# Unread products in TensorE's planned gaps, single-slot weight decoding and a newly set order in a fused attention and feed-forward kernel

## The chip, the cores and the metric

The kernel runs on one core of one Trainium2 chip. The metric is the device time of one execution in microseconds (us); for the kernel before it is given as the median of three runs. The core's engines run side by side, each through its own list of instructions in order: TensorE (products), VectorE, ScalarE, GpSimd, and SyncE (SP), which issues all transfers here. They meet at semaphores.

## The reference

The input is 4 batches of 8 heads, 576 positions, 64 values per head. Three parts follow each other:

```
scores = q k^T / 8 - slope_h * |i - j|,  kept where 0 <= i - j < 128
x      = softmax(scores) v                       -> 2304 tokens x 512
h      = x w_in (512 x 1024);  e = softmax(h);  s = h * e
ln     = (s - mean(s)) / sqrt(var(s) + 1e-6) * g_ln
y      = ln w_out (1024 x 512)
h2     = y w2_in (512 x 2048);  g = h2 * sigmoid(h2)
out    = g w2_out (2048 x 512)
```

The weights arrive as 64-bit floats, 8 bytes for each value: w_in is 4.2 MB, w_out 4.2 MB, w2_in and w2_out 8.4 MB each.

## The kernel before

**Tiling.** The 2304 tokens are 18 blocks of 128. A block runs through attention in four pairs of heads: scores (`a_qk`, L615), bias and row maximum on VectorE (`a_max`, L640), exponentials on ScalarE (L645), a split of the result into a high and a low 16-bit half, a transpose, and the product with v (`a_av`, L692). `a_evac` gathers the block's 128x512 result `xm`, which is split and transposed into `xT`. `m1_in` (L734) multiplies by w_in, `layer_norm` does both normalisations, and every second block `m1_out` (L826) multiplies 256 tokens by w_out into `y16`. A pair of blocks is a chunk `c`; its last part is eight steps `j` of `m2_in` (L863), a gate (ScalarE L872, VectorE L873, ScalarE L875, VectorE L876, into a buffer `g`), and `m2_out` (L890). Every large product is made of three 16-bit products (high by high, high by low, low by high).

**Weights.** A weight is loaded in slots of 128 x 512 values, 48 in all: 8 of w_in, 8 of w_out, 16 of w2_in, 16 of w2_out. `load_weight` takes two slots at a time: two loads of 512 KB into one of `N_STAGE` = 2 stage buffers, then `decode`, three VectorE operations over 1024 elements that build 32-bit floats out of the two halves of the 64-bit ones (L414, L416, L418). The intermediate `bits` lies in PSUM, in the pool `ps_early`, two banks wide. Per slot, ScalarE (or GpSimd) squares the result and, save for w2_out, TensorE sums over partitions with a matrix of ones (L459); from the sums comes one scale for a weight. `split_weight` then makes the two 16-bit halves of each slot, by one of three ways given in the string `E_W`: V (ScalarE, VectorE L482), G (ScalarE, ScalarE, GpSimd) or H (GpSimd L487, ScalarE, GpSimd). All slots of a weight must be decoded before its scale is known. The first `m2_in` needs all of w2_in, the first `m2_out` all of w2_out.

**Transposes.** The string `ON_PE` says for each block whether the transposes of attention weights ("a"), of `xm` ("x") and of the LayerNorm result ("l") are made by TensorE (P: products with the unit matrix L520, ScalarE L522, VectorE L523) or by transfers (D: a ScalarE copy L335 or L790, a difference on VectorE L339 or GpSimd L340, transposing transfers). `ENG` says which engine takes those differences (V, G, or B for whichever ends sooner by the plan) and the normalisation ("n", V or A for VectorE L774 or ScalarE L772).

**Order.** All instructions are first recorded as `Op` objects with their dependences, a cost and a priority. `Sched.solve` then walks through a planned time: it takes the engine that can begin first and gives it the ready operation of the lowest priority number. That fixes the order on each engine and the order of buffer use; the chip then follows that order, waiting where an operand is late. The priorities come from tables: `RANK` and `PITCH` by kind and block, `WAT` by weight. The constants `N_...` say how many buffers of each kind rotate; `AHEAD` says how many steps `m2_in` is recorded ahead of `m2_out`. The planned costs are fixed numbers, with one speed for TensorE.

Of the kernel before, what the change touches and what calls it, by code (L numbers as in the profile page):

```python
# [7 lines left out]
F32 = mybir.dt.float32  # L8
# [3 lines left out]
U32 = mybir.dt.uint32  # L12
# [5 lines left out]
P = 128  # L18
# [52 lines left out]

class Sched:
    def __init__(self):
        self.ops, self.state, self.prio, self.pred = [], {}, 0.0, {}

    def at(self, kind, i, p=0):

# [100 lines left out]
    def solve(self):  # L178
# [34 lines left out]
        while n_left:  # L213
            while todo:
                o = todo.pop()
                if o.eng is None and o.turn is not None and o.fn is not None:
                    o.turn.waiting.append(o)
                    n_left -= give(o.turn)
                elif o.eng is None:
                    o.start = o.end = o.ready  # L220
                    n_left -= 1
                    settle(o)
                    if o.turn is not None:
                        turn = o.turn
                        turn.done[o.buf.place] = o.end
                        while len(turn.released) - turn.n in turn.done:
                            turn.released.append(turn.done.pop(len(turn.released) - turn.n))
                        n_left -= give(turn)
                else:
                    for alt in o.alts:  # L230
                        avail[alt[0]].append((o, alt))
            if not n_left:
                break
            best = None
            for e, lst in avail.items():
                lst[:] = [x for x in lst if not x[0].done]
                if not lst:
                    continue
                t = max(free[e], min(o.ready for o, _ in lst))
                if best is None or t < best[0]:  # L240
                    best = (t, e)
            assert best is not None, "tiles wait for each other"
            t, e = best
            o, alt = min((x for x in avail[e] if x[0].ready <= t), key=lambda x: (x[0].prio, x[0].idx))

            for other in o.alts:
                begins = max(free[other[0]], o.ready, port if other[3] else 0)
                if begins + other[1] < max(t, port if alt[3] else 0) + alt[1]:
                    alt = other
            o.eng, o.cost, o.fn, held = alt  # L250
            t = max(free[o.eng], o.ready, port if held else 0)
            o.done, o.start = True, t
            free[o.eng] = t + o.cost
            if held:
                port = t + o.cost
            if o.dma:
                dma_free = max(dma_free, t + (1100 if o.cost < 600 else 1275)) + o.dma
                o.end = dma_free
            else:
                o.end = free[o.eng]  # L260
            n_left -= 1
            settle(o)
# [33 lines left out]
def fused_kernel(ctx, tc, qk, qn, kn, vt, rel, w_in, w_out, g_ln, w2_in, w2_out, out):  # L296
# [71 lines left out]

    def over_partitions(x, n, first=False):

        pt = Buf(ps_early, [P, 1024], F32, "bits", 1) if first else Buf(ps, [P, 512], F32, "mm", 2, free=True)
        pe(220, lambda: T.matmul(pt[:, 0:n], ones.tile, x.tile, start=True, stop=True), [ones, x], [pt])
        return pt


    def norm_scale(name, parts, n=None):
# [24 lines left out]
        return big, scl  # L401


    def decode(st, slots):

        t = Buf(ps_early, [P, 2, 512], U32, "bits", 1)

        def flat(x):
            return x.rearrange("p a c -> p (a c)")

        def out():
            return W.tile.bitcast(U32)[:, slots[0]:slots[1] + 1:slots[1] - slots[0], :]
        w = [(W, sl) for sl in slots]
        v(1050, lambda: V.tensor_scalar(flat(t.tile), flat(st[:, :, :, 1]), 3, 0x3FFFFFFF, ALU.logical_shift_left,  # L414
                                        ALU.bitwise_and), [st], [t])
        v(1050, lambda: V.scalar_tensor_tensor(out=flat(t.tile), in0=flat(st[:, :, :, 1]), scalar=0xC0000000,  # L416
                                               in1=flat(t.tile), op0=ALU.bitwise_and, op1=ALU.bitwise_or), [st, t], [t])
        v(1050, lambda: V.scalar_tensor_tensor(out=out(), in0=st[:, :, :, 0], scalar=29, in1=t.tile,  # L418
                                               op0=ALU.logical_shift_right, op1=ALU.bitwise_or), [st, t], w)

    scales, sums = {}, {}

    def load_weight(name, w, slot0, n, cols, gain=None, columns=False, by_rows=False):
# [2 lines left out]
        groups = n if by_rows else nf if columns else 1  # L426
        acc = Buf(const, [P, groups], F32, "acc" + name)
        view = w.bitcast(U32).rearrange("(k p) (f e) -> p k f e", p=P, f=nf)
        for at in range(0, n, 2):
            s.prio = WEIGHT(slot0, at) - 8  # L430
            st = Buf(early, [P, 2, 512, 2], U32, "stage", N_STAGE)
            slots = []
            for z in range(2):
                f, k = divmod(at + z, n // nf)
                slots.append(slot0 + LAG + k * nf + f)
                load(512, lambda f=f, k=k, z=z, st=st: SP.dma_start(st[:, z].rearrange("p c e -> p (c e)"),
                                                                    view[:, k, f, :]), [], [(st, z)])
            s.prio = WEIGHT(slot0, at)
            decode(st, slots)

            def go(at, k, sl):
                if by_rows:
                    junk = Buf(early, [P, 512], BF16, "sq", 2)
                    act(512, lambda: A.activation(junk.tile, W[:, sl, :], AF.Square, accum_out=acc[:, at:at + 1]),
# [16 lines left out]
                if at % size == size - 1:  # L461
                    v(512, lambda: V.tensor_reduce(acc[:, at // size:at // size + 1], c.tile, AX.X,
                                                   ALU.max if columns else ALU.add), [c], [(acc, at // size)])
            for z in range(2):
                go(at + z, (at + z) % (n // nf), slots[z])
        scales[name] = norm_scale(name, acc, None if by_rows else groups)

    def split_weight(name, slot0, n, cols, per_k=None):
# [484 lines left out]
    n = 0  # L953
    for c in range(NB // 2 + 1):
# [16 lines left out]

PITCH = 3.3
RANK = {"table": -104.3, "vnorm": -66.9, "vload": 632.4, "vsplit": 82.3, "load": -243.6, "qk": -57.4,
        "max": -161.5, "exp": 217.8, "parts": -218.7, "aturn": -111.4, "av": 179.9, "evac": -188.6,
        "xturn": -57.5, "in": -119.2, "max1": 91.3, "norm": -233.0, "lparts": -421.0, "out": -334.0,
        "share": -317.7, "y": -192.5, "in2": 186.3, "gate": -449.4, "out2": 257.1, "store": -337.1}

WAT = {0: (65.8, 0.0, 85.1, 0.0), 8: (-155.1, 0.0, -336.6, 0.0), 16: (49.3, 0.0, 5.2, 0.0),
       32: (144.1, 0.0, -16.4, 0.0)}


def WEIGHT(slot0, at, split=False):
# [4 lines left out]
LAG = 2  # L992
NSLOT = 48
TB = 256
E_W = "GHGVHGVHGVVGVVHGVHVHVGGVGVGGGGGVHGVGHHVGHVGGHVVH"

ENG = {"n": "VAAAAAVVVVVAAAAAAA", "a": "GGGGGGGGVVVVVVVBVV", "x": "BGGGGVGBBBBBGGGBBB",
       "l": "VBBGGGGGBBBBBBGVVV"}

ON_PE = {"a": "DDDDPDDDDDDDDDDDDD", "x": "PDPDPPDDDDDDDDDDDD", "l": "DPDDDDDDDDDDDDDDDD"}  # L1000
N_STAGE = 2
N_VS = 2
N_VRAW = 2
N_K = 2
N_Q = 2
N_E = 2
N_A16 = 2
N_AT = 2
N_XT = 1
N_E1 = 1  # L1010
N_L16 = 1
N_LNT = 1
N_Y = 1
N_T = 6
N_G = 5
AHEAD = 1
SKEW = 0
NQ = NB
V_AT = [0, 1, 5, 9]

# [1 line left out]
_INS = ["qk", "qn", "kn", "vt", "rel", "moe_w_in", "moe_w_out", "moe_g_ln", "moe2_w_in", "moe2_w_out"]  # L1022
# [50 lines left out]
```

## Time and profile before

| quantity | value |
| --- | --- |
| median of 3 runs | 750.63 us (747.43 to 752.69) |
| profiled execution, its own time | 750.25 us |
| its span, first to last instruction | 748.5 us |
| mean granted TensorE clock | 0.962 of full |
| TensorE products: busy, share, count | 685.3 us, 92%, 5382 |
| VectorE: busy, share, count | 450.9 us, 60%, 1167 |
| ScalarE: busy, share, count | 400.5 us, 54%, 850 |
| GpSimd: busy, share, count | 111.7 us, 15%, 96 |

Busy time is the sum of an engine's instructions on the chip, not of its waiting. TensorE's products are pipelined and may overlap, so a group of several takes less time than its count times the mean of one. The granted clock is the share of full speed that the chip allows TensorE. In the rows, PE is TensorE, DVE is VectorE, ACT is ScalarE, POOL is GpSimd; `sa<-k,q` reads "writes tile sa from tiles k and q"; what stands in brackets or after `<-` with a line number is the instruction waited for. A row of the table of stretches gives, for each engine, busy us and in brackets the number of instructions that began there.

### The profile page before, as it was taken

The numbers are of one execution on the slowest core, as the hardware profiler recorded it, in microseconds if no ns is written. First come the engines' busy times: TensorE is split into PE (matmuls) and PEld (weight loads), VectorE is DVE, ScalarE is ACT, GpSimd is POOL, SyncE is SP. The second block draws the span as 40 slices with busy tenths as digits, with TensorE's granted clock in tenths as the row PEclk, the third lists the DMA queues.
The fourth block names the chain that finished last, engine by engine and source line by source line (L and its number), as shares of the span: only waits on it lengthen the run. The fifth ranks groups of instructions, "written<-read, shape, count | busy, mean of one in ns | idle before, by whom it ended". The sixth has DMA issues, their size and how long they took to land.

```text
span 748.5 us, 13814 instructions
## 1 busy us (share of the span) xinstructions
PE 685.3 (92%) x5382; PEld 458.8 (61%) x5382; DVE 450.9 (60%) x1167; ACT 400.5 (54%) x850; POOL 111.7 (15%) x96
## 2 busy tenths in 40 slices
PE   2475777989999999999999999999999999999998
PEld 1233344776766558765666677757667767857853
DVE  3899899989868884887716655641552362222220
ACT  5597758998598864666714464431432352232231
POOL 2075321443276110100000100000100000000000
PEclk9996757899999999999999999999999999999999
DMA  9899996477864652847612235121210300200000
GB/s 244 281 301 235 221 258 207 140 156 173 167 122 107 146 125 51 151 105 152 154 29 43 62 81 85 29 57 23 42 36 15 57 29 4 54 29 1 2 28 29
DMA packets 139809, 79.22 MB, mean 106 GB/s; under 512 B 121696, under 2 KB 122336, under 8 KB 139744
## 3 DMA queue, kind: packets, MB, share of 16 engines
q1 hardware_dynamic: 139744, 78.34, 44.6%
q8 instruction: 42, 0.69, 0.4%
q14 instruction: 23, 0.19, 0.1%
HBM read 44.24 MB, written 4.72 MB: 65 GB/s over the span
## 4 chain that ended last, share of the span: by engine, by line
PE 80%; DVE 8%; DMA 5%; ACT 3%; issue 2%; POOL 1%; SPq 0%; DVEq 0%; ACTq 0%
PE mm L890 25%; PE mm L863 23%; PE mm L826 13%; PE mm L734 11%; PE sa L615 4%; PE sa L692 3%; DVE bits L416 1%; DVE W L418 1%; DVE e L640 1%; DMA stage<-in_moe_w_out_dram 1%; DVE bits L414 1%; DMA stage<-in_moe_w_in_dram 1%; DMA k<-in_kn_dram 1%; DMA lnT<-ln 1%; DMA aT<-a 1%
## 5 line engine op out<-in xcount | busy, mean ns | idle before, releaser
L863 PE MATMUL mm<-y,W 128*128 128x256 f16 x1728 | 210.4, 273 | 1.8 <-DVE t L873 1.8
L890 PE MATMUL mm<-W,g 128*128 128x512 f16 x864 | 207.5, 379 | 0.0
L863 PEld LDWEIGHTS <-W 128*128 128x128 f16 x1728 | 165.9, 98 | 39.3 <-issue 2.6
L890 PEld LDWEIGHTS <-g 128*128 128x128 f16 x864 | 82.5, 98 | 74.9 <-issue 0.2
L826 PE MATMUL mm<-lnT,W 128*128 128x256 f16 x864 | 110.0, 277 | 2.3 <-DVE aT L523 1.5
L734 PE MATMUL mm<-W,xT 128*128 128x512 f16 x432 | 103.2, 391 | 2.4 <-DVE W L482 0.9
L826 PEld LDWEIGHTS <-W 128*128 128x128 f16 x864 | 84.5, 99 | 22.8 <-DVE aT L523 1.8
L645 ACT ACTIVATE e<-e,mx 128x256 f32<-128x256 f32 (+1 forms) x144 | 70.1, 488 | 43.1 <-DVE mx L640 38.4
L876 DVE SCALAR_TENSOR_TENSOR g<-t,g 128x512 f16<-128x512 f32 x72 | 50.9, 708 | 59.9 <-ACT g L875 59.7
L875 ACT ACTIVATE g<-t 128x512 f16<-128x512 f32 x72 | 45.1, 627 | 75.8 <-PE mm L890 63.5
L872 ACT ACTIVATE t<-mm,cs 128x512 f32<-128x512 f32 x72 | 48.7, 679 | 60.1 <-PE mm L863 59.9
L873 DVE SCALAR_TENSOR_TENSOR t<-t,mm 128x512 f32<-128x512 f32 x72 | 48.9, 683 | 51.3 <-ACT t L872 50.9
L615 PE MATMUL sa<-k,q 64*128 64x128 f32 x544 | 58.4, 335 | 20.9 <-DVE mx L640 14.9
L734 PEld LDWEIGHTS <-xT 128*128 128x128 f16 x432 | 42.4, 100 | 52.8 <-issue 8.8
L615 PEld LDWEIGHTS sa<-k,q 64*128 64x128 f32 x544 | 42.7, 214 | 46.6 <-DVE mx L640 25.9
L640 DVE CUSTOM_DVE_ANT_0 e<-sa,table 128x256 f32<-128x256 f32 (+1 forms) x144 | 55.1, 401 | 26.5 <-PE sa L692 13.8
L692 PEld LDWEIGHTS <-aT 128*128 128x128 f16 x816 | 33.8, 102 | 20.7 <-DMA aT<-a 9.4
L692 PE MATMUL sa<-vs,aT 128*128 128x64 f16 x816 | 37.9, 200 | 8.5 <-DMA aT<-a 4.8
L335 ACT ACTIVATE a<-e 128x512 f16<-128x512 f32 (+1 forms) x68 | 40.3, 597 | 8.7 <-DMA aT<-a 7.8
L834 DVE SCALAR_TENSOR_TENSOR y<-mm,cs,y 128x512 f16<-128x512 f32 x18 | 13.5, 750 | 49.2 <-ACT y L831 49.2
L340 POOL TENSOR_TENSOR a<-e,a 128x512 f16<-128x512 f32 (+1 forms) x28 | 31.1, 1114 | 75.3 <-ACT a L335 74.7
L340 POOL TENSOR_TENSOR W<-W 128x512 f16<-128x512 f32 x31 | 37.7, 1230 | 25.8 <-ACT W L335 25.8
(133 smaller groups left out, 685.5 us busy)
## 6 DMA issues: line engine op xcount, KB each, us to landing
stage<-in_moe_w_in_dram SPq DMA_DIRECT2D x24, 512.0 KB, 6.0
stage<-in_moe_w_out_dram SPq DMA_DIRECT2D x24, 512.0 KB, 4.9
vraw<-in_vt_dram SPq DMA_DIRECT2D x34, 256.0 KB, 4.0
k<-in_kn_dram SPq DMA_DIRECT2D x18, 256.0 KB, 2.9
q<-in_qn_dram SPq DMA_DIRECT2D x18, 256.0 KB, 3.4
out_dram<-t SPq DMA_DIRECT2D x18, 256.0 KB, 2.0
aT<-a SPq DMA_TRANSPOSE x68, 3.5
lnT<-ln SPq DMA_TRANSPOSE x34, 3.2
```

The source lines that it names most:

```text
L340: "G": ("G", cg(n), lambda: G.tensor_tensor(dst(), a(), b(), op), True)}
L615: T.matmul(SA[:, j, sl * P:(sl + 1) * P], q[rows, p, :], k[rows, p, :], start=True, stop=sl not in blank)
L640: v(n + 20, lambda j=j: V.tensor_tensor_reduce(e[:, j, lo:lo + n], SA[:, j, lo:lo + n], table[:, 2 * p + j, o:o + n], -0.125, 3.0e38, ALU. ...
L645: act(n, lambda j=j: A.activation(e[:, j, lo:lo + n], e[:, j, lo:lo + n], AF.Exp, bias=mx[:, j:j + 1], scale=-1.0, accum_out=rs[:, 2 * p + ...
L692: T.matmul(heads()[:, h // 4, h % 4, :], t[:, (2 * ha + j) * nh + c, :], vb[sl][:, h, hv, :], start=(n == 0), stop=(n == 3 * nh - 1))
L734: T.matmul(pt[:, half * 512:(half + 1) * 512], x[:, hx, k, :], W16(2 * k + half, hw), start=(k == 0 and hx + hw == 0), stop=(k == KD - 1 a ...
L826: T.matmul(pt[:, ct % 2], W16(8 + k, hw)[:, ct * P:(ct + 1) * P], l[:, hx * KF1 + k, :], start=(k == 0 and hw + hx == 0), stop=(k == KF1 - ...
L863: T.matmul(pt[:, mm], W16(16 + 4 * k + m // 4, hw)[:, (m % 4) * P:(m % 4 + 1) * P], y[:, hx, k, :], start=(k == 0 and hw + hx == 0), stop= ...
L872: act(512, lambda: A.activation(t.tile, flat(pt.tile), AF.Tanh, scale=cs[:, 0:1]), [pt, (cs, 0)], [t], extra=1)
L873: v(512, lambda: V.scalar_tensor_tensor(out=t.tile, in0=t.tile, scalar=1.0, in1=flat(pt.tile), op0=ALU.add, op1=ALU.mult), [t, pt], [t])
L876: v(512, lambda: V.scalar_tensor_tensor(out=flat(g[:, 1]), in0=t.tile, scalar=2.0 ** -16, in1=flat(g[:, 0]), op0=ALU.mult, op1=ALU.subtrac ...
L890: T.matmul(pt.tile, g[:, hg, mm, b * P:(b + 1) * P], W16(32 + m, hw), start=(m == 0 and hg + hw == 0), stop=(m == KF2 - 1 and hg == 1))
```

## The change

`solve` gets a filler. Where TensorE's next planned operation begins more than 360 ns after the last one ends, it puts products of 160 ns planned time into the gap, each a matrix of ones by 384 columns of the bias table, into a bank `idle` that is never read; only between 14 and 135 us of planned time. Weights are decoded slot by slot: one load, three VectorE operations over 512 elements, `bits` one bank wide; the bank given up is `idle`. `N_STAGE` becomes 3 buffers of half the size. The tables of priorities, the engine strings and the numbers of buffers are set anew.

```diff
 class Sched:
-        self.ops, self.state, self.prio, self.pred = [], {}, 0.0, {}
+        self.ops, self.state, self.prio, self.pred, self.filler = [], {}, 0.0, {}, None
...
             t = max(free[o.eng], o.ready, port if held else 0)
+            if o.eng == "PE" and self.filler:
+                fn, buf, (begin, end, gap) = self.filler
+                x = max(free["PE"], begin)
+                while x + gap < min(t, end):
+                    f = Op((("PE", 160, fn, False),), 0, len(self.ops))
+                    f.eng, f.cost, f.fn = "PE", 160, fn
+                    f.start, f.end = x, x + 160
+                    order.append(f)
+                    x += 160
...
-        pt = Buf(ps_early, [P, 1024], F32, "bits", 1) if first else Buf(ps, [P, 512], F32, "mm", 2, free=True)
+        pt = Buf(ps_early, [P, 512], F32, "bits", 1) if first else Buf(ps, [P, 512], F32, "mm", 2, free=True)
...
+    idle = Buf(ps_early, [P, 512], F32, "idle", 1)
+    s.filler = (lambda: T.matmul(idle[:, :3 * P], ones.tile, table[:, 0, :], start=True, stop=True), idle, FILL)
...
-    def decode(st, slots):
-        t = Buf(ps_early, [P, 2, 512], U32, "bits", 1)
...
-        v(1050, lambda: V.tensor_scalar(flat(t.tile), flat(st[:, :, :, 1]), 3, 0x3FFFFFFF, ALU.logical_shift_left,
-                                        ALU.bitwise_and), [st], [t])
...
+    def decode(st, sl):
+        t = Buf(ps_early, [P, 512], U32, "bits", 1)
+        v(512, lambda: V.tensor_scalar(t.tile, st[:, :, 1], 3, 0x3FFFFFFF, ALU.logical_shift_left,
+                                       ALU.bitwise_and), [st], [t])
+        v(512, lambda: V.scalar_tensor_tensor(out=t.tile, in0=st[:, :, 1], scalar=0xC0000000, in1=t.tile,
+                                              op0=ALU.bitwise_and, op1=ALU.bitwise_or), [st, t], [t])
+        v(512, lambda: V.scalar_tensor_tensor(out=W[:, sl, :].bitcast(U32), in0=st[:, :, 0], scalar=29, in1=t.tile,
+                                              op0=ALU.logical_shift_right, op1=ALU.bitwise_or), [st, t], [(W, sl)])
...
-        for at in range(0, n, 2):
-            st = Buf(early, [P, 2, 512, 2], U32, "stage", N_STAGE)
+        for at in range(n):
+                st = Buf(early, [P, 512, 2], U32, "stage", N_STAGE)
+                load(512, lambda: SP.dma_start(st.tile.rearrange("p c e -> p (c e)"), view[:, k, f, :]), [], [st])
+                decode(st, sl)
...
-PITCH = 3.3
-RANK = {"table": -104.3, "vnorm": -66.9, "vload": 632.4, "vsplit": 82.3, "load": -243.6, "qk": -57.4,
-        "max": -161.5, "exp": 217.8, "parts": -218.7, "aturn": -111.4, "av": 179.9, "evac": -188.6,
-        "xturn": -57.5, "in": -119.2, "max1": 91.3, "norm": -233.0, "lparts": -421.0, "out": -334.0,
-        "share": -317.7, "y": -192.5, "in2": 186.3, "gate": -449.4, "out2": 257.1, "store": -337.1}
-WAT = {0: (65.8, 0.0, 85.1, 0.0), 8: (-155.1, 0.0, -336.6, 0.0), 16: (49.3, 0.0, 5.2, 0.0),
-       32: (144.1, 0.0, -16.4, 0.0)}
+PITCH = 4.97
+RANK = {"table": -102.1, "vnorm": 36.7, "vload": 424.7, "vsplit": -53.8, "load": -121.4, "qk": -82.0,
+        "max": -49.1, "exp": 275.4, "parts": -273.2, "aturn": -68.2, "av": 137.6, "evac": -309.3,
+        "xturn": -302.2, "in": -252.9, "max1": 65.4, "norm": -154.9, "lparts": -445.6, "out": -180.2,
+        "share": -370.7, "y": -115.0, "in2": 44.4, "gate": -242.7, "out2": 166.7, "store": -203.8}
+WAT = {0: (70.8, 0.0, 124.5, 0.0), 8: (-123.5, 0.0, -241.4, 0.0), 16: (28.8, 0.0, 102.9, 0.0),
+       32: (126.1, 0.0, -0.7, 0.0)}
...
-E_W = "GHGVHGVHGVVGVVHGVHVHVGGVGVGGGGGVHGVGHHVGHVGGHVVH"
-ENG = {"n": "VAAAAAVVVVVAAAAAAA", "a": "GGGGGGGGVVVVVVVBVV", "x": "BGGGGVGBBBBBGGGBBB",
-       "l": "VBBGGGGGBBBBBBGVVV"}
-ON_PE = {"a": "DDDDPDDDDDDDDDDDDD", "x": "PDPDPPDDDDDDDDDDDD", "l": "DPDDDDDDDDDDDDDDDD"}
-N_STAGE = 2
+E_W = "HGHHHGGGVGGVHGVVVVHGHHGGVGGGGGVGVVGGGVHHVVHHGVHH"
+ENG = {"n": "VVVAAAAAAVVAVVVVVA", "a": "GGGGGGGGGGBBGGBBGB", "x": "VGGGGGGVBVBVBBGGVV",
+       "l": "GBBBBBBBGGGGGGBBVV"}
+ON_PE = {"a": "DDDDDDDDDDDDDDDDDD", "x": "PDPPDDDDDDDDDDDDDD", "l": "DPDPPDDDDDDDDDDDDD"}
+N_STAGE = 3
...
-N_Q = 2      -N_E = 2      -N_A16 = 2   -N_AT = 2    -N_XT = 1
+N_Q = 1      +N_E = 3      +N_A16 = 1   +N_AT = 3    +N_XT = 3
-N_Y = 1      -N_T = 6      -N_G = 5     -AHEAD = 1
+N_Y = 2      +N_T = 7      +N_G = 3     +AHEAD = 2
...
+FILL = (14000, 135000, 360)
```

## Rows read from the trace of the kernel before

**Rows 1.** the page's 40 slices of 18.7 us: busy tenths, and the granted clock
```profile
PE   2475777989999999999999999999999999999998
...
DVE  3899899989868884887716655641552362222220
...
PEclk9996757899999999999999999999999999999999
```

**Rows 2.** the table of stretches: the first row names the columns
```profile
core 0: us, PE busy (x) PEld busy (x) DVE busy (x) ACT busy (x) POOL busy (x), PEclk, DMA share, GB/s
0.00:30.00 30.00, 9.57 (x46) 5.62 (x47) 15.87 (x44) 17.17 (x53) 5.32 (x16) 1.00 0.89 258
30.00:130.00 100.00, 67.43 (x479) 37.60 (x477) 94.27 (x225) 74.14 (x170) 37.63 (x31) 0.76 0.94 250
130.00:205.00 75.00, 69.68 (x639) 53.13 (x640) 67.43 (x160) 61.63 (x140) 29.19 (x24) 0.96 0.70 159
205.00:500.00 295.00, 293.94 (x2505) 194.97 (x2503) 192.67 (x563) 172.61 (x378) 37.48 (x25) 1.00 0.46 95
```

**Rows 3.** TensorE's order of time: start, us taken, line, tiles, count
```profile
22.59 1.23 PE L615 MATMUL sa<-k,q 64*128 64x128 f32 x8
...
130.46 13.28 PE L826 MATMUL mm<-lnT,W 128*128 128x256 f16 x96 [1.49 <-DVE aT L523]
...
187.26 0.72 PE L615 MATMUL sa<-k,q 64*128 64x128 f32 x8 [0.18 <-DVE mx L640]
```

**Rows 4.** waits of VectorE, first 30 us: total us, times, longest
```profile
DVE bits L414 <- DMA stage<-in_moe_w_in_dram: 3.4, 3, 2.7
DVE e L640 <- PE sa L615: 3.0, 2, 2.0
```

**Rows 5.** waits of VectorE, 30 to 130 us
```profile
DVE e L640 <- PE sa L692: 3.4, 2, 2.5
DVE e L640 <- PE sa L621: 0.8, 1, 0.8
DVE bits L414 <- DMA stage<-in_moe_w_out_dram: 0.6, 1, 0.6
```

**Rows 6.** the chain that ended last, in order of time: start, us, what
```profile
624.87 6.55 PE mm L826 x60
```

**Rows 7.** the table of stretches again, another cut
```profile
14.00:135.00 121.00, 79.15 (x534) 44.92 (x535) 112.42 (x279) 88.13 (x207) 44.04 (x38) 0.78 0.91 244
```

**Rows 8.** VectorE's order of time, around 61 us and 70 us
```profile
61.05 1.22 DVE L414 TENSOR_SCALAR bits<-stage 128x1024 uint32<-128x1024 uint32 x1
62.30 1.23 DVE L416 SCALAR_TENSOR_TENSOR bits<-stage,bits 128x1024 uint32<-128x1024 uint32 x1
63.44 0.68 DVE L462 TENSOR_REDUCE accwout<-mm 128x1 f32<-128x512 f32 x1
64.04 0.69 DVE L705 TENSOR_TENSOR xm<-sa,rinv 128x512 f32<-128x512 f32 x1
...
69.59 0.75 DVE L482 SCALAR_TENSOR_TENSOR W<-W,gs 128x512 f16<-128x512 f32 x1
70.26 1.22 DVE L416 SCALAR_TENSOR_TENSOR bits<-stage,bits 128x1024 uint32<-128x1024 uint32 x1
```

**Rows 9.** groups by line and shape: total us, mean ns, idle before
```profile
L339 DVE TENSOR_TENSOR ln<-e,ln 128x1024 f16<-128x1024 f32 x11 | 13.5, 1223 | 25.7 <-ACT ln L790 25.7
...
L482 DVE SCALAR_TENSOR_TENSOR W<-W,sw2in 128x512 f16<-128x512 f32 x6 | 5.2, 861 | 0.0
...
L774 DVE TENSOR_SCALAR e<-e,lnst 128x1024 f32<-128x1024 f32 x6 | 4.9, 811 | 0.1
...
L487 POOL TENSOR_SCALAR W<-W,swin 128x512 f32<-128x512 f32 x3 | 4.6, 1564 | 0.9 <-DVE swin L400 0.9
...
L523 DVE TENSOR_TENSOR aT<-mm,aT 128x512 f16<-128x512 f32 x4 | 2.7, 683 | 0.2 <-ACT aT L522 0.2
...
L482 DVE SCALAR_TENSOR_TENSOR W<-W,swin 128x512 f16<-128x512 f32 x2 | 2.4, 1192 | 0.0
```

More of the change, by code (lines that the diff above doesn't have):

```diff
@@ L401, in norm_scale @@
         return big, scl
-    def decode(st, slots):
-        t = Buf(ps_early, [P, 2, 512], U32, "bits", 1)
[L408 to L413, printed above, removed]
-        v(1050, lambda: V.tensor_scalar(flat(t.tile), flat(st[:, :, :, 1]), 3, 0x3FFFFFFF, ALU.logical_shift_left,
-                                        ALU.bitwise_and), [st], [t])
[L416 to L419, printed above, removed]
+    def decode(st, sl):
[6 more added lines that the diff above has]
+                                              op0=ALU.logical_shift_right, op1=ALU.bitwise_or), [st, t], [(W, sl)])
     scales, sums = {}, {}
@@ L428, in load_weight, with go @@
         view = w.bitcast(U32).rearrange("(k p) (f e) -> p k f e", p=P, f=nf)
-        for at in range(0, n, 2):
-            s.prio = WEIGHT(slot0, at) - 8
-            st = Buf(early, [P, 2, 512, 2], U32, "stage", N_STAGE)
[L432 to L441, printed above, removed]
+        for at in range(n):
+            f, k = divmod(at, n // nf)
+            def go(k=k, f=f, at=at, sl=slot0 + LAG + k * nf + f):
+                s.prio = WEIGHT(slot0, at) - 8
+                st = Buf(early, [P, 512, 2], U32, "stage", N_STAGE)
+                load(512, lambda: SP.dma_start(st.tile.rearrange("p c e -> p (c e)"), view[:, k, f, :]), [], [st])
+                s.prio = WEIGHT(slot0, at)
+                decode(st, sl)
                 if by_rows:
@@ L463, in go @@
                                                    ALU.max if columns else ALU.add), [c], [(acc, at // size)])
-            for z in range(2):
-                go(at + z, (at + z) % (n // nf), slots[z])
+            go()
         scales[name] = norm_scale(name, acc, None if by_rows else groups)
@@ L1004 @@
 N_K = 2
[L1005 to L1009, printed above, removed]
+N_Q = 1
+N_E = 3
+N_A16 = 1
+N_AT = 3
+N_XT = 3
 N_E1 = 1
@@ L1012 @@
 N_LNT = 1
[L1013 to L1016, printed above, removed]
+N_Y = 2
+N_T = 7
+N_G = 3
+AHEAD = 2
 SKEW = 0
```

## The prediction

> **What bounds the kernel now.** I read the page's forty slices first. TensorE is short of work until about slice 9 and full from there to the end; VectorE is the reverse [rows 1]. The table of stretches puts numbers on it [rows 2]: TensorE is busy 9.57 us of the first 30, 67.43 of the next 100, 69.68 of the 75 after that, and then 293.94 of 295. VectorE is busy 94.27 us of the 100 from 30 to 130. So there are two regimes. From about 130 us on, TensorE sets the time, and its work there is fixed by the sizes. Before that, VectorE sets it: it decodes weights and serves attention, and TensorE takes what it is handed. The end moves only if more TensorE work is behind us when the second regime starts, or if it starts earlier.
>
> The same table shows the clock. [...]
>
> The profiled execution took 750.25 us, of which the span is 748.5; the median of the runs is 750.63, so the sum holds for the median within 0.4 us. One per cent, about what a measurement can tell from no change, is 7.5 us.
>
> **The parts, one by one.**
>
> Clock. [...] In the first 30 us that is 3.0 us (scores) [rows 4]; from 30 to 130 us it is 3.4 + 0.8 = 4.2 us [rows 5]. At full clock a score group loses 0.51 of 1.23 us, two fifths, but a saved moment also lets later work through earlier. I take 1 of the 3.0 and 3 of the 4.2 (bounds: nothing, and all 7.2). Where TensorE is already the bound, the clock counts in full: the first 96 products of m1_out took 13.28 us from 130.46 us on [rows 3], and 60 later ones 6.55 us, so 10.48 for 96 [rows 6]: 2.8 us, taken whole. Together -6.8.
>
> Fillers. A product of 384 columns costs, from 6.55/60 for 256 columns, 0.164 us at full clock and twice that at half. TensorE is idle 121 - 79.15 = 41.9 us between 14 and 135 us [rows 7], room for 255 of them, and for more once the products shrink. They need no operand that is late and write a bank that nobody reads. Laid into planned gaps they cost nothing as long as the true gap is as long; the cover is VectorE's being late. If it is gone, see the first rival. In the sum: 0 (bounds 0 and +11).
>
> Decoding slot by slot. Two pairs of numbers stand in VectorE's order of time [rows 8]. A decode operation over 1024 starts 1.25 us before one that depends on it (61.05 to 62.30) and 1.14 before one that does not (62.30 to 63.44); one over 512 is followed after 0.60 us (63.44 to 64.04) or 0.67 (69.59 to 70.26). Three operations over a pair take 3.42 us when other work stands between them and 3.64 when they follow each other (twice 1.25, once 1.14). Six over 512 take 3.6 (0.60 each) to 4.3 (0.67, and 0.11 more for the four that depend on the one before). The difference is 0.18 us at least and 0.65 with the ends crossed; for the 16 pairs of w_in, w_out and w2_in that is 3 to 10 us before TensorE is full. I take 5, nearer to the low end, because the order often puts other work between. [...] For the other eight pairs the price falls later, where TensorE is already nearly full, and I take none. In return the first decode needs one transfer landed, not two: VectorE waited 3.4 us for weights in the first 30 [rows 4]; I take 2 (bounds 0 and 3.4). Three stage buffers of one slot hold less ahead than two of two, but after that start VectorE waited for weights 0.6 us in 100 [rows 5], so 0. The loads were single slots before; their number on SP's queue is unchanged.
>
> Who does what. VectorE's part of the weight splits falls by two slots in w_in (1.19 us each), two in w2_in (0.86 each), one more in w2_out, late. Block 4's transposed weights leave TensorE and so four conversions of 0.68 on VectorE. Block 0's LayerNorm difference goes from VectorE (1.22) to GpSimd. Two more blocks are normalised on VectorE (0.81 each), and block 3's LayerNorm transposes come to TensorE (two conversions of 0.68) [rows 9]. Sum: -2.4 - 1.7 - 2.7 - 1.2 + 1.6 + 1.4 = -5.0 (bounds -5 and 0, should the other engines be late instead). On the transfer queue block 4 adds four transposes and block 5 one, block 3 takes one plus two away and block 4 two: nothing net. GpSimd is busy 37.63 of 100 us [rows 2], and gets one pre-scaling more in w_in (1.56) and two more differences; that chain leads to the first m1_in, which is covered while VectorE still has w_out to decode. If not, +4.
>
> Buffers and order. Deeper xT, aT, e and y, shallower q, a16 and g. The gaps of TensorE between 130 and 205 us are 75 - 69.68 = 5.3 us; I take -1 (bounds +5 and -5). Afterwards m2_in runs two steps ahead of m2_out instead of one, so each gate has a step more time, and three g buffers hold those two and the one being read; with one step ahead TensorE lost 1.06 us in 295 [rows 2]. The late regime keeps its length, with 4 transposes less in 5382 products.
>
> **Sum:** -6.8 + 0 + 5 - 2 - 5 - 1 = -9.8, 750.25 - 9.8 = 740 us.
>
> **Rivals.**
>
> First, slower: the fillers stand in front of real work. TensorE takes its queue in order, so a score product that is ready earlier than planned waits for the rest of its gap; VectorE stands behind it with its whole queue, the decode included. Price: where TensorE was full (130 to 205) VectorE idled 7.6 of 75 us, in 30 to 130 only 5.7 of 100 [rows 2]. At the former rate the 121 us of filling cost 12.2 instead of 6.9, so 5.4 more; as planned times also miss, I double it: 11 us, and without the gains 761 us. For it: nearly all gaps get filled, and the queue cannot pass over. Against: VectorE runs at its limit, so its answers come late rather than early, and score groups shrink by 0.5 us. It decides when VectorE's idle time from 30 to 130 us exceeds about 10 us. With dearer decoding (+5) it reaches 766.
>
> Second, nothing: VectorE is so full that the warm clock only lengthens TensorE's true idling, and the extra 72 decode operations eat the lighter splits. Then only the 2.8 us of the burst and 2 at the start are left, against +5 more from decoding: about 750 us, 744 to 757. For it: 94.27 us busy in 100. The case in which fillers do not hold the clock at all (the 360 ns left in each gap, products waiting besides) ends here too.
>
> Third, more: every favourable bound at once, because the new order lets finer pieces fill VectorE's idle time. That is -10.0 for the clock (7.2 + 2.8), +3 for decoding, -3.4 for the first load, -5.0 for the shift of work and -5.3 for TensorE's gaps: -20.7, so 729.6 us. For it: VectorE still idles 14.1 us in the first 30. Against: the page shows few waits that end on something the change touches, and the weights of the first two stages, which the change still decodes on VectorE, come first in any order.
>
> **Numbers.** Forecast (732 to 743) 0.43; more (below 732) 0.09; nothing (743 to 758) 0.28; slower (over 758) 0.20. The time is the forecast's, 740. The range 722 to 759 holds the forecast, the second rival and the third, with 7 us for what an order set anew may find besides; outside lie 0.02 below and most of the slower rival above, some 0.17. The forecast's own range is 732 to 743. Faster by over 1% (below 743): 0.43 + 0.09 = 0.52; within 1%: 0.28; slower: 0.20.
>
> **What would show it.** Right: clock 0.9 or more from 30 to 130 us; eight scores in about 0.75 us from 20 us on; the first 96 products of m1_out in under 11 us and starting no later than 130 us; VectorE over 93% busy before that; TensorE full afterwards. Decode operations over 512 of 0.64 to 0.75 us. Wrong: TensorE full of fillers while VectorE waits on scores (first rival); m1_out starting after 135 us at full clock (second); starting before 120 us (third); TensorE gaps after 205 us, which would mean that the shallower g or a16 binds.

## The result, and the profile after

The changed kernel takes 755.06 us (median; 752.91 to 756.11) against 750.93 for the kernel before on the same chips: a ratio of 1.0057 with an interval of 1.0044 to 1.0071, slower by 4 us and so within 1%. The forecast was 740, faster by over 1%. The stated range of 722 to 759 holds the time; the direction was wrong. The profiled execution took 753.98 us with a span of 752.2, 3.7 us more than the span before, and its granted clock is 1.000.

The page's slices after (busy tenths in 40 slices, then the granted clock) answer to [rows 1]:

```profile
PE   4998988888999999999999999999999999999997
DVE  5899999899887555545554444575447545321221
PEclk9999999999999999999999999999999999999999
```

TensorE now looks full from the second slice on, and the granted clock reads 0.9 or more in all 40 slices. (Lines of after are two higher than before's for the products: scores L617, attention weights times v L694, m1_in L736, m1_out L828. The decode is L421, L423, L425, the a16 copy on ScalarE L344, the difference on GpSimd L349.) The table of stretches, with the columns of [rows 2], shows what it is full of; the second fence is the same table for the unread products alone.

```profile
0.00:30.00 30.00, 19.21 (x120) 11.04 (x121) 18.99 (x55) 18.99 (x56) 3.66 (x14) 1.00 0.87 259
30.00:130.00 100.00, 89.63 (x698) 50.33 (x697) 93.78 (x244) 68.39 (x152) 41.36 (x34) 1.00 0.93 238
130.00:205.00 75.00, 67.54 (x623) 50.07 (x621) 70.12 (x192) 62.93 (x148) 33.91 (x28) 1.00 0.73 171
205.00:500.00 295.00, 292.95 (x2433) 199.09 (x2430) 167.21 (x490) 160.97 (x341) 59.12 (x44) 1.00 0.38 80
```

```profile
30.00:130.00 100.00, 50.26 (x271) 25.45 (x270) 1.00 0.93 238
```

From 30 to 130 us, 50.26 of TensorE's 89.63 us are unread products; the real work is the other 39.4 us (427 products), where it was 67.43 at the lower clock (479 products). VectorE is as busy as before (93.78 against 94.27). Behind 130 us TensorE idles more than before: 7.5 us against 5.3 in 75, and 2.05 against 1.06 in 295 [rows 2].

TensorE's order of time answers to [rows 3]:

```profile
22.40 0.71 PE L617 MATMUL sa<-k,q 64*128 64x128 f32 x8
...
63.44 0.72 PE L617 MATMUL sa<-k,q 64*128 64x128 f32 x8
...
128.87 10.19 PE L828 MATMUL mm<-lnT,W 128*128 128x256 f16 x90
139.07 5.34 PE L736 MATMUL mm<-W,xT 128*128 128x512 f16 x24
144.25 0.82 PE L828 MATMUL mm<-lnT,W 128*128 128x256 f16 x6
...
148.48 0.51 PE L694 MATMUL sa<-vs,aT 128*128 128x64 f16 x12 [1.88 <-DVE mx L642]
```

Eight scores take 0.71 us at 22 us already. The first m1_out begins at 128.87 instead of 130.46, and 90 of its products take 10.19 us, where 96 took 13.28; the last six come behind an m1_in. VectorE's waits, in total us, times and longest, answer to [rows 4, 5]; first those of the first 30 us, then those from 30 to 130:

```profile
DVE nrmb L403 <- PE mm L381: 1.1, 1, 1.1
DVE e L642 <- PE sa L617: 1.0, 1, 1.0
DVE bits L421 <- DMA stage<-in_moe_w_in_dram: 0.5, 1, 0.5
DVE e L642 <- PE sa L694: 0.4, 1, 0.4
```

```profile
DVE xm L707 <- PE sa L694: 2.2, 2, 1.6
...
DVE bits L421 <- DMA stage<-in_moe_w_out_dram: 0.6, 1, 0.6
...
DVE e L642 <- PE sa L617: 0.4, 1, 0.4
```

The waits before `e` that I wanted to see go mostly went: from 3.0 to 1.4 us in the first 30 and from 4.2 to 0.4 in the next 100. Others on TensorE came, 1.1 us before `nrmb` and 2.2 before `xm`; all of VectorE's waits on TensorE in these 130 us are 5.1 us, and were 7.2. The groups by line and shape answer to [rows 8, 9]:

```profile
L423 DVE SCALAR_TENSOR_TENSOR bits<-stage,bits 128x512 uint32<-128x512 uint32 x48 | 33.2, 693 | 0.5
L421 DVE TENSOR_SCALAR bits<-stage 128x512 uint32<-128x512 uint32 x48 | 33.1, 689 | 1.8 <-DMA stage<-in_moe_w_in_dram 0.8 <-DMA stage<-in_moe_w_out_dram 0.6
L425 DVE SCALAR_TENSOR_TENSOR W<-stage,bits 128x512 uint32<-128x512 uint32 x48 | 32.8, 683 | 0.7
```

Every mark that I named for "right" is there but the last, TensorE full afterwards, and the kernel is slower. To see where the time went I counted, in both traces, the real products still to come at a given moment and priced each kind at its mean spacing at full speed (256 columns 6.55/60 = 0.109 us [rows 6], 512 columns 0.216, a score 0.077, a product of attention weights and v 0.029, a transpose 0.125). What is left of the span beyond that work is loss.

| from the first m1_out to the end | before | after |
| --- | --- | --- |
| it begins at | 130.5 us | 128.9 us |
| span still to run | 618.0 | 623.3 |
| real work still to do | 597.2 | 599.7 |
| the rest: gaps, slow clock | 20.8 | 23.6 |

After starts this regime 1.6 us earlier, but with 2.5 us more work in front of it (24 more products of attention weights, 8 more scores, 8 more transposes) and 2.8 us more loss, although 2.8 of before's loss was the slow clock of the burst (the table reads 0.50 from 128 to 132 us, 0.51 from 132 to 136 and 1.00 from 136 to 140): 2.5 + 2.8 - 1.6 = 3.7, the difference of the spans. Attention also ends later: the last scores run at 569 us instead of 446, and from 300 to 600 us TensorE is busy 297.51 us against 299.70. That the late gaps come from the long attention is read from the traces, not tested.

### The profile page after: what moved, and what is told of

Same layout as the page of the kernel before. It is cut to its first block, busy times and chain, and to the rows that moved or that the text cites. A ratio compares the mean times of both kernels' runs of the same rounds, so it can differ in the third digit from the quotient of the medians.

```text
span 752.2 us, 14513 instructions
## 1 busy us (share of the span) xinstructions
PE 717.2 (95%) x5707; PEld 476.9 (63%) x5707; DVE 451.1 (60%) x1206; ACT 400.1 (53%) x855; POOL 148.3 (20%) x127
## 4 chain that ended last, share of the span: by engine, by line
PE 71%; DMA 8%; DVE 8%; ACT 7%; POOL 3%; issue 2%; SPq 0%; POOLq 0%; DVEq 0%; ACTq 0%
PE mm L892 24%; PE mm L865 21%; PE mm L828 11%; PE mm L736 9%; DMA aT<-a 5%; PE sa L617 3%; PE sa L694 2%; POOL a L349 1%; DMA lnT<-ln 1%; DVE e L642 1%; ACT a L344 1%; PE idle L387 1%; ACT W L344 1%; DVE bits L421 1%; POOL W L489 1%
## 5 line engine op out<-in xcount | busy, mean ns | idle before, releaser
L349 POOL TENSOR_TENSOR a<-e,a 128x512 f16<-128x512 f32 (+1 forms) x55 | 61.2, 1112 | 331.5 <-ACT a L344 331.2
L828 PE MATMUL mm<-lnT,W 128*128 128x256 f16 x864 | 103.3, 273 | 0.0
L736 PE MATMUL mm<-W,xT 128*128 128x512 f16 x432 | 98.0, 379 | 1.2 <-DMA xT<-x 0.7
L828 PEld LDWEIGHTS <-W 128*128 128x128 f16 x864 | 83.0, 98 | 17.7 <-issue 0.5
L736 PEld LDWEIGHTS <-xT 128*128 128x128 f16 x432 | 41.8, 98 | 50.1 <-issue 2.2
L642 DVE CUSTOM_DVE_ANT_0 e<-sa,table 128x256 f32<-128x256 f32 (+1 forms) x144 | 54.6, 402 | 20.8 <-POOL a L349 9.1
L387 PE MATMUL idle<-table,ones 128*128 128x384 bf16 x329 | 62.9, 333 | 0.0
L617 PE MATMUL sa<-k,q 64*128 64x128 f32 x544 | 51.8, 305 | 10.5 <-DVE mx L642 5.4
L344 ACT ACTIVATE a<-e 128x512 f16<-128x512 f32 (+1 forms) x72 | 43.0, 598 | 34.0 <-DMA aT<-a 33.8
L617 PEld LDWEIGHTS sa<-k,q 64*128 64x128 f32 x544 | 37.5, 190 | 31.3 <-DVE mx L642 10.9
L387 PEld LDWEIGHTS <-ones 128*128 128x128 bf16 x329 | 31.4, 99 | 27.4 <-issue 8.2
L750 DVE TENSOR_REDUCE lnst<-mm 128x1 f32<-128x1024 f32 x18 | 22.0, 1222 | 40.6 <-PE mm L736 40.5
L349 POOL TENSOR_TENSOR W<-W 128x512 f16<-128x512 f32 x34 | 41.1, 1221 | 10.3 <-ACT W L344 10.3
```

Of the source, the lines that this page charges most:

```text
L344: "A": ("A", ca(n), lambda: A.activation(dst(), src(), AF.Copy), False)}
L349: "G": ("G", cg(n), lambda: G.tensor_tensor(dst(), a(), b(), op), True)}
L387: s.filler = (lambda: T.matmul(idle[:, :3 * P], ones.tile, table[:, 0, :], start=True, stop=True), idle, FILL)
L617: T.matmul(SA[:, j, sl * P:(sl + 1) * P], q[rows, p, :], k[rows, p, :], start=True, stop=sl not in blank)
L642: v(n + 20, lambda j=j: V.tensor_tensor_reduce(e[:, j, lo:lo + n], SA[:, j, lo:lo + n], table[:, 2 * p + j, o:o + n], -0.125, 3.0e38, ALU. ...
L736: T.matmul(pt[:, half * 512:(half + 1) * 512], x[:, hx, k, :], W16(2 * k + half, hw), start=(k == 0 and hx + hw == 0), stop=(k == KD - 1 a ...
```

## The experiments

All ratios are against the kernel before; to put one in us, multiply by 751.

### The unread products alone

**e1** is the changed kernel without them; every other engine's list is the same.

```diff
-    s.filler = (lambda: T.matmul(idle[:, :3 * P], ones.tile, ...), idle, FILL)
+    s.filler = None
```

> The changed kernel with its order and its decoding, without the 329 unread products. Three theories. A, absorbed: VectorE bounds the first 130 us, so a full clock mostly lengthens TensorE's waits, and the 72 extra decode operations use up what is left; B, obstruction: the unread products hold up real ones; C, tables: the new priorities, engine strings and buffer numbers are the worse ones. A: the clock falls to about 0.76 between 30 and 130 us again, and the time rises by what the full clock is worth where TensorE is the bound, 2 to 6 us: ratio 1.009 to 1.014. B: it falls to or below that of the kernel before: ratio 0.995 to 1.001. C says nothing of this run beyond what A says.

Measured: 755.26 us, 1.0062 [1.0049, 1.0074], level with after: the ratios differ by 0.0005, give or take 0.0018 (1.4 us). The stretch from 30 to 130 us of e1, its first m1_out, and VectorE's two longest waits in that stretch:

```profile
30.00:130.00 100.00, 61.85 (x414) 32.66 (x414) 91.44 (x240) 67.76 (x151) 40.58 (x34) 0.74 0.91 235
```

```profile
129.68 11.30 PE L828 MATMUL mm<-lnT,W 128*128 128x256 f16 x90
```

```profile
DVE xm L707 <- PE sa L694: 3.3, 2, 2.6
DVE e L642 <- PE sa L617: 2.2, 1, 2.2
```

The clock falls to 0.74, and the real work takes 61.85 us instead of 39.4. The 22 us saved by the fast clock were idle time that TensorE had anyway. VectorE does wait less for TensorE with the products, 5.1 us in the first 130 against 7.4 in e1, but m1_out begins at 128.9 us with them and at 129.7 without. The burst is 1.1 us slower in e1 (11.30 us against 10.19), and in the 75 us after 130 after idles 7.5 us where e1 idles 6.1: most of that lead came back as waiting. The wait on scores in the first 30 us is 1.0 us in e1 as well, so its fall from 3.0 belongs to the new order and not to the clock.

**e11** narrows the products to 128 columns.

```diff
-T.matmul(idle[:, :3 * P], ones.tile, table[:, 0, :], ...)
+T.matmul(idle[:, :P], ones.tile, table[:, 0, :P], ...)
```

> The changed kernel with its 329 unread products at 128 columns instead of 384: they hold TensorE a third as long. B, obstruction cancels the clock: if the clock still holds above 0.9 from 30 to 130 us, the time falls by 2 us or more, ratio 0.999 to 1.004. If neither is worth anything (e1 was level because TensorE is not the bound there at either clock): ratio 1.005 to 1.007, whatever the clock does.

Measured: 755.39 us, 1.0052 [1.0033, 1.0071]; clock 0.86 from 30 to 130 us. A third setting of the clock, with products that are busy for 32.5 us in all instead of 62.9, and the same time.

**e17** puts two products where after puts one, 658 in all.

```diff
                     order.append(f)
+                    order.append(f)
```

> The changed kernel with each of the 329 unread products made twice, 658 in all, 54 us more of TensorE's time at full clock. If the gaps on the chip are longer than planned and hide single ones entirely, the price of the second 329 shows how much room was left: with no room, up to 50 us more; ratio 1.02 to 1.07. If they hardly hold anything up because nothing of the early stage waits for TensorE, under 5 us: 1.005 to 1.012.

Measured: 793.06 us, 1.0560 [1.0541, 1.0579]. The stretch from 30 to 130 us, and VectorE's longest wait from 30 to 160:

```profile
30.00:130.00 100.00, 99.37 (x723) 59.07 (x722) 67.66 (x172) 52.87 (x119) 35.14 (x30) 1.00 0.68 173
```

```profile
DVE e L643 <- PE sa L695: 18.9, 6, 6.8
```

This is the first rival as I had drawn it: TensorE full, VectorE idle 32 us of 100 and waiting for products. The second set costs 38 us for 54 us of products (329 at 0.164), so the first set had left some 16 us of the gaps.

### The grain and the order

**e2** decodes slot by slot under before's tables, strings and buffers, with four single stage buffers and no unread products; **e3** adds those products (314).

```diff
-PITCH = 4.97 ... (all tables, strings and buffer counts of after)
+PITCH = 3.3 ...  (those of before, N_STAGE = 4)
```

> The tables, engine strings and buffer numbers of the kernel before, no unread products, and only the decoding slot by slot (four stage buffers of one slot, as many bytes as before). A: 144 decode operations over 512 instead of 72 over 1024, 3 to 10 us more on VectorE before TensorE is full: ratio 1.004 to 1.012. B and C: decoding is not the cost, ratio 0.998 to 1.002.

> As the run before, with some 314 unread products in the gaps of that plan, 14 to 135 us. A: a few us below the run before and about level with the kernel before: ratio 0.998 to 1.006. B: above the run before by 3 us or more. C: clearly better than the changed kernel, ratio 0.990 to 0.998, since the tables are the good ones.

Measured: e2 775.02 us, 1.0329 [1.0316, 1.0343]; e3 770.02, 1.0263 [1.0244, 1.0282]. Finer decoding under the old priorities costs 24 us, five times what I had put down; the new tables, strings and buffer counts together win 20 of it back (e2 to e1; no run separates the three). The place is the stretch from 130 to 205 us of e2, where TensorE starves:

```profile
130.00:205.00 75.00, 57.99 (x464) 39.06 (x462) 70.41 (x196) 60.19 (x137) 29.02 (x22) 0.83 0.64 170
```

The scale of w2_in, before which none of its products can run, is ready at 159.6 us instead of 127.7. VectorE's load alone does not explain that: the last slot of w2_in is decoded at 134.5 us instead of 118.8, and the squares and sums of its last slots run only at 151 to 155 us, behind other work. In this order the unread products are worth 5 us: VectorE's waits on TensorE in the first 130 us fall from 8.5 to 5.9 us, and w2_in's scale, on which TensorE then waits, is ready 4.9 us sooner. So what a full clock is worth depends on the order.

### VectorE's load, in an unchanged order

**e4** is after, **e7** is before; in both the middle decode operation gives way to an empty step of the same planned cost, so the lists stay as they are; the last operation takes over its work, and the lowest 3 bits of each weight are left out.

```diff
-        v(512, lambda: V.scalar_tensor_tensor(out=t.tile, ..., scalar=0xC0000000, ...), [st, t], [t])
-        v(512, lambda: V.scalar_tensor_tensor(out=W..., in0=st[:, :, 0], scalar=29, ...), ...)
+        v(512, lambda: None, [st, t], [t])
+        v(512, lambda: V.scalar_tensor_tensor(out=W..., in0=st[:, :, 1], scalar=0xC0000000, ...), ...)
```

> The changed kernel in its own order, with two decode operations a slot instead of three: the lowest 3 bits of each 32-bit weight are left out, so the middle operation falls away on VectorE. 48 operations of 0.69 us, started 0.60 to 0.72 us apart; 32 of them lie before TensorE is full, about 20 us of VectorE. A: that stage shortens by most of it, time falls by 10 to 20 us: ratio 0.979 to 0.992. B and C: VectorE's load is not what decides, the fall stays under 5 us: ratio 0.999 to 1.006.

> The kernel before, its order, its pairs, with two decode operations a pair instead of three (lowest 3 bits of each weight left out): 24 operations of 1.22 us fall away on VectorE, 16 of them before TensorE is full, some 19 us. If VectorE bounds the kernel before (which has two a16 buffers), the time falls by 10 us or more: ratio 0.976 to 0.987. If the transfers or the order bound it as well, by 2 to 6 us: 0.992 to 0.997.

Measured: e4 750.11 us, 0.9995 [0.9981, 1.0009]; e7 746.91, 0.9953 [0.9936, 0.9970]. The stretch from 30 to 130 us of e4:

```profile
30.00:130.00 100.00, 90.81 (x706) 52.66 (x703) 79.24 (x225) 69.29 (x158) 43.97 (x35) 0.98 0.91 240
```

VectorE is relieved of 14.5 us in this stretch alone and of 28.4 in all (25.6 in e7), and the end moves 4 to 5 us: about 0.15 us for each. The stretch is not VectorE's alone.

### What else holds the first 130 us

After's chain of waits (start, us, what) shows a ring that before's did not:

```profile
85.34 0.64 ACT a L344
...
86.11 1.18 POOL a L349
...
87.30 3.02 DMA aT<-a
...
90.34 0.64 ACT a L344
...
91.11 1.17 POOL a L349
...
92.29 4.79 DMA aT<-a
...
97.10 0.63 ACT a L344
```

With one a16 buffer the next copy on ScalarE waits until the transpose by transfer has read the last one. ScalarE's wait of that kind in after, over the span:

```profile
ACT a L344 <- DMA aT<-a: 33.8, 24, 3.9
```

Before, with two buffers, it was 7.8 us in 8 waits. **e5** gives after two real a16 buffers with the plan unchanged; **e6** and **e8** do so on top of e4, with the unread products and without.

```diff
-tag=x.tag, bufs=x.n, name=x.tag
+tag=x.tag, bufs=2 if x.tag == "a16" else x.n, name=x.tag
```

> The changed kernel, its order to the instruction, but the 16-bit attention weights a16 get two buffers on the chip where the plan reckons with one. New theory D: in the changed order the early stage runs in a ring (ScalarE copy, GpSimd difference, transposing transfer, and the next copy, which waits until the transfer has read the one buffer); that ring, not VectorE, sets the pace from 40 to 130 us. D: ScalarE's 33.8 us of waiting on the transfer vanish, the first m1_out starts 3 to 10 us earlier, ratio 0.990 to 1.002. A (VectorE alone): no more than 1 us, ratio 1.004 to 1.007.

> The run before and, on top, two decode operations a slot instead of three (the lowest 3 bits of each 32-bit weight left out). D: two bounds lie side by side, each hides the other, so both together give clearly more than the sum of the single gains: ratio 0.975 to 0.988. A: as the two operations alone, 0.998 to 1.001.

> As e6, without the unread products. With both other bounds moved away, TensorE's clock should come to matter: if the full clock was worthless only because others were slower, this run is 3 to 8 us slower than e6. If unread products hold up as much as the clock gives, the two are level within 1.5 us.

Measured: e5 753.87 us, 1.0040 [1.0024, 1.0057]; e6 748.65, 0.9981 [0.9966, 0.9995]; e8 748.50, 0.9968 [0.9951, 0.9985]. In e5 the wait falls from 33.8 to 2.0 us, the end by about 1, with intervals that overlap; a long chain of one kind is not yet a price. e8 against e6 says again that the products and the clock together are worth nothing measurable, now with VectorE relieved.

**e9** loads half of each weight into the same buffers, and decodes it twice; the other half is left out.

```diff
-SP.dma_start(st.tile..., view[:, k, f, :])
+SP.dma_start(st.tile...[:, 0:512], view[:, k, f, 0:512])
```

> The changed kernel in its order; each weight load fetches only the first 256 of the 512 columns, and the decode reads those twice (so half of each weight is left out; the number and size of the VectorE operations stay). 24 loads of 512 KB and 24 more become half, 12.6 MB less of the 44 that are read. The transfer engines were busy 0.93 from 30 to 130 us. Theory E, transfers: they set the early pace, so the first m1_out starts 8 us or more earlier and the ratio is 0.975 to 0.993. If the transfers are only one of several, 1 to 4 us: 0.999 to 1.005. If they are not a bound, 1.005 to 1.007.

Measured: 751.03 us, 0.9997 [0.9984, 1.0010]: the transfers' share from 30 to 130 us falls from 0.93 to 0.68, and the end by 4 us. **e14** has all three reliefs (e6 and e9 together), **e16** the same without unread products.

> The changed kernel in its order with three burdens moved away together: two a16 buffers, two decode operations a slot (3 bits left out), half loads (half of each weight left out). If the early stage is a mesh of VectorE, transfers and the attention ring, where each is hidden by the others, the sum of the single gains (5 + 1 + the gain of half loads) is exceeded by 5 us or more: ratio below 0.985. If the order itself holds things up, with engines waiting in turn for each other, the gains only add up: 0.988 to 0.998.

> As e14 (two a16 buffers, two decode operations, half loads, half of each weight left out), without the unread products. TensorE was busy 95 of 100 us from 30 to 130 us in e14, mostly with them. If they now stand in front of real work, the time falls by 2 us or more: ratio below 0.991. If the clock is worth something at last, it rises by 2 us or more: above 0.997. If neither, 0.992 to 0.996.

Measured: e14 746.92 us, 0.9940 [0.9918, 0.9961]; e16 744.78, 0.9919 [0.9906, 0.9932]. The three together give 8 us where one by one they gave 1, 5 and 4: no one of them was the bound, and none hid behind another. The stretch from 30 to 130 us of e16:

```profile
30.00:130.00 100.00, 65.37 (x466) 37.63 (x466) 80.59 (x227) 71.34 (x160) 48.57 (x38) 0.80 0.67 165
```

Nothing in it is full, and m1_out still begins only at 121.6 us, 8 sooner than in e1. That the fixed order and the passing from engine to engine are what remains is read from this, not tested.

### The order, with nearly the same instructions

**e12** and **e13** have the work of e7 and e4, but the planner is told that the dropped operation is gone and orders anew. The instructions are not quite the same: in e12 two copies go from ScalarE to VectorE and one square from GpSimd to ScalarE, in e13 three copies go from ScalarE to VectorE, and e13 gets 362 unread products where e4 has 329. **e15** is e7 with a second xT and a third a16 buffer.

```diff
-        v(1050, lambda: None, [st, t], [t])
```

> The kernel before with two decode operations a pair (lowest 3 bits of each weight left out), and this time the plan knows of it, so that the order is new. If orders are worth what the plan says, below e7: ratio 0.985 to 0.994. If a table of priorities only fits the kernel it was set for, as e2 suggests (24 us lost by a changed grain under the old tables), it is worse than e7 by 4 us or more: ratio above 1.000.

> The changed kernel's tables with two decode operations a slot (3 bits left out), and the plan knows of it; the instructions are those of e4, only their order is new. Theory O, order: once no single engine sets the pace, the order in which the engines meet decides by many us. O: it differs from e4 by 4 us or more either way: ratio below 0.994 or above 1.005. If the order is worth little: 0.997 to 1.002.

> As e7 (the kernel before, its order, two decode operations, 3 bits left out), with a second xT buffer and a third a16 buffer on the chip that the plan does not reckon with. If buffers hold the old order up, 2 to 5 us less than e7: ratio 0.988 to 0.993; if not, 0.994 to 0.997.

Measured: e12 758.10 us, 1.0089 [1.0064, 1.0113]; e13 752.50, 1.0023 [1.0010, 1.0036]; e15 747.07, 0.9950 [0.9937, 0.9963]. The plan that knows more is 11 us slower than e7, and 2 slower than e4, although w2_out's scale is ready 39 and 36 us earlier. By the count of products, e12 has 601.1 us of real work left at 130 us and e7 595.7 (24 more scores and 36 more products of attention weights among it): weights were brought forward, mostly at the price of attention. That is 5.4 of the 12.8 us between the two spans; the other 7.4 are gaps and slow clock behind 130 us, 3.5 of them from 300 to 500 us; first e12, then e7:

```profile
300.00:500.00 200.00, 196.10 (x1705) 130.01 (x1703) 126.07 (x357) 107.39 (x233) 3.85 (x3) 1.00 0.47 88
```

```profile
300.00:500.00 200.00, 199.56 (x1692) 132.46 (x1691) 123.83 (x346) 103.32 (x217) 4.00 (x4) 1.00 0.42 84
```

e15 is level with e7: these two buffers are not what holds the old order. e6, e7, e8, e14, e15 and e16 end below both kernels; all leave out part of the decoding, as their expectations say, so no faster version with the full result came of this.

## Why the prediction was wrong

**The step that failed** stands in its first paragraph: "Before that, VectorE sets it". From it each microsecond saved on VectorE, or in VectorE's waits, was booked as nearly one microsecond of time. It holds for about a seventh of one (e4, e7). VectorE was 94% busy, but so was the transfer share, and behind both stood chains from engine to engine in a fixed order. Before's chain of waits, summed by engine from 30 to 130 us, runs 46.5 us through VectorE, 19.0 through TensorE, 14.1 through transfers and 11.8 through ScalarE; after's runs 28.1 through VectorE and 1.2 through TensorE, e1's 20.3 through TensorE, and after and e1 take the same time, as they would if chains of nearly equal length lie side by side. Relieving VectorE, the loads or the a16 ring gives 1 to 5 us each.

**Clock, -6.8 forecast, nothing measured** (e1, e8, e11). That products which nobody reads hold the clock up was an assumption of mine; the runs show 0.74 without them and 1.00 with them from 30 to 130 us. Of the 3.0 and 4.2 us that VectorE waited for TensorE [rows 4, 5] I took 1 and 3. No run shows the 1 us for the first 30 us, where I had gone by the 1.23 against 0.72 us of eight scores [rows 3]: the wait on scores there is 1.0 us in after and in e1. The first half of the mechanism came as drawn: clock 1.00, scores in 0.72 us, a burst of 10.19 us for 90 products, VectorE's waits on TensorE 2.3 us shorter than in e1. But a wait that goes from VectorE came back as another wait, and the 2.8 us that I "took whole" were not whole either: by e1 the products shorten the burst by 1.1 us, and TensorE was last in the burst alone and not in the 75 us around it, where it idled 5.3. Under the old tables (e2, e3) the same products do pay, 5 us; so the term is not nothing by itself, but in this order. In after's order nothing followed from the higher clock: 755.26 us without the products (e1), 755.06 with them.

**Fillers, 0, bounds 0 and +11: as forecast** at the single size, though e1 shows only their price and the clock's gain together. VectorE idles 6.2 us from 30 to 130, below the 10 from which the first rival decides; e17 shows that rival at the double size. Whether a little obstruction cancels a little gain from the clock stays open: e16 is 2 us below e14, with intervals that just overlap.

**Decoding slot by slot, +5.** The durations came out inside 0.64 to 0.75 us (means of 683 to 693 ns), and VectorE's decoding rose from 87.7 to 99.1 us: 11.4 us for 24 pairs, so 7.6 for 16, where I took 5. My upper end was added up wrong: six operations at 0.67 us and four times 0.11 are 4.46 us, not 4.3, so 0.82 a pair and 13 us for 16, not 10. As load the 11.4 us are worth about 1.7 us by the rate of e4 and e7. As a change of grain under tables set for another it is worth 24 (e2), which the sum had nowhere.

**First load, -2:** VectorE's wait for w_in fell from 3.4 to 0.5 us, and w_in's scale was ready at 40.2 us instead of 39.8. Nothing came through.

**Who does what, -5.0:** booked at full price; by the same rate less than 1 us. I had also counted only what moves off VectorE and not that GpSimd goes from 111.7 to 148.3 us of work, and left out block 4's LayerNorm transposes, which come to TensorE too (the conversions of `lnT` on VectorE go from 2 to 6, not to 4).

**Buffers and order, -1 with bounds of 5 either way:** the size was off by far. The new tables, strings and buffer counts take 20 us off (e2 to e1), and an order set anew adds 11 with nearly the same instructions (e12). The sum with the grain, +24 - 20 = +4, is the result; the two were one choice, and I priced them as separate and small. Of the 14 us between forecast and result, about 7 are the clock's (-6.8 against nothing) and about 7 lie here: grain, first load, who does what and order were to give -3 and gave +4.5 (e1). The late mark, gaps after 205 us, showed: 2.05 us against 1.06; I had laid it to shallower g or a16. With two a16 buffers (e5) it is still 1.98 us, so it is not a16; g was not tested.

**The second rival** had the time (744 to 757) and half the reason: the full clock did only lengthen TensorE's idling, now filled (from 30 to 130 us the real work takes 39.4 us at 1.00 and 61.85 at 0.74 in e1). But it was not VectorE alone that was full, m1_out did not start after 135 us, and the loss sits behind that point: more work left, and more gaps.

## What to carry to other kernels

What a full clock is worth has to be measured in the order at hand: here 1.00 against 0.74 from 30 to 130 us gave nothing (755.06 against 755.26 us), and under the old tables the same kind of products gave 5 us (e2, e3). Products that fill TensorE's idle time bought a better clock reading, and past the true gaps they cost time (38 us for 54 us of them, e17). An engine that is 94% busy is a bound only if taking work off it in the same order moves the end (28.4 us off VectorE moved it by 5, e4), so price a microsecond by that before summing any. Where an order is set by tables, a change of grain and the tables are one edit, and the measure of an order is how much of the last engine's work is done by a moment and how few gaps follow, not how early a weight is ready (w2_out's scale was 39 us earlier in e12 than in e7, and the time 11 us longer).

## What the runs showed of the hardware besides

Operations of VectorE and GpSimd that ran side by side were often longer than alone. The group `vs` of VectorE takes 1070 ns on average after and 768 before, with the same shapes, and the scores' group 416 in both. One `vs` at 44.70 us took 1.67 us; the second fence is GpSimd at that time (start, us):

```profile
44.70 1.67 DVE L582 SCALAR_TENSOR_TENSOR vs<-vraw,sv,vs 128x512 f16<-128x512 f32 x1
...
188.46 0.74 DVE L582 SCALAR_TENSOR_TENSOR vs<-vraw,sv,vs 128x512 f16<-128x512 f32 x1
```

```profile
43.55 2.28 POOL L349 TENSOR_TENSOR W<-W 128x512 f16<-128x512 f32 x2
...
188.55 1.68 POOL L349 TENSOR_TENSOR x<-xm,x 128x512 f16<-128x512 f32 x1
```

At 44.70 VectorE's operation takes 0.93 us more than at 188.46; there it keeps its 0.74, and GpSimd's takes 1.68 where most of its kind take 1.15 to 1.17. Of the 18 operations of the group `vs` after, the eight with nothing running on GpSimd took 0.70 to 0.75 us, and nine of the other ten 1.06 to 1.68. In before five of the 18 ran beside a named operation of GpSimd: three took 0.74 us, one 0.84 and one 1.12. So the longer times stand beside work of the other engine, for either engine but not in every pair; the cause was not shown, and no run isolated it.

The granted clock from 30 to 130 us was 0.74 without the unread products (e1), 0.86 with products of 128 columns (e11) and 1.00 with 384 (after). In the first 30 us the column reads 1.00 before and after, while eight scores at 22 us took 1.23 us [rows 3] and 0.71 us: there the durations differ, and the column does not. Later in before the two agree: eight scores took 1.22 us at 65.59 us, where the column reads 0.50 (64 to 68 us), and 0.72 at 85.19, where it reads 1.00 (84 to 88).
